# A two-stage attention and feed-forward kernel: softmax steps, the order of block sums, and the product scheme of three blocks

## The chip, the cores and the metric

One core of a Trainium2 chip runs the whole kernel. The metric is the device time of one execution in microseconds; times in the profile count from the first instruction.

## The reference

```python
def _attn_ref(q, k, v, tau):                      # q, k, v: (4, 6080, 256)
    qn = q / (np.linalg.norm(q, axis=1, keepdims=True) + 1e-06)
    kn = k / (np.linalg.norm(k, axis=1, keepdims=True) + 1e-06)
    s = kn.transpose(0, 2, 1) @ qn / tau          # 256 x 256 for each batch
    s = s - s.max(-1, keepdims=True)
    a = np.exp(s)
    a /= a.sum(-1, keepdims=True) + 1e-09
    return (v @ a).astype(np.float32)

def _moe_ref(x, w_in, w_out):                     # 256 -> 2048 -> 256
    h = np.maximum(x @ w_in, 0.0)
    return (h * h @ w_out).astype(np.float32)
```

The output is `_moe_ref` of the attention's 24320 rows.

## The kernel before

Attention here is over channels: each batch needs one 256 x 256 matrix `a` from its q and k, and `v @ a @ w_in` is computed as `v @ W` with W = `a @ w_in` made once for each batch. So a batch has an attention part (products of q and k into `gram`, sums of squares into `acc`, the softmax, W) and a feed-forward part over its tokens. The attention part of batch b + 1 is put between the steps of the feed-forward part of batch b.

**Feed-forward.** A batch's 6080 tokens are 11 blocks of 512 and one of 448. For each block, 16 steps f (128 hidden channels each) run `first_product` (line 541): six matmuls of the block's width into a PSUM tile `ps_h` (three buffers), since each float32 operand is split into a high and a low fp32r part and three of the four part products are kept, over two halves of the channels. ScalarE (ACT) applies relu into a tile `x`. Two steps make a pair r. At the odd step, `squares_and_sums` (line 565) squares the pair on ACT.

In blocks for which `by_seven` (line 534) is true, the pair is taken as a 2 x 2 arrangement of blocks, x[0] to x[3] (two hidden channel groups by two halves of the tokens), and the second product, with `w_out` arranged 2 x 2 likewise, takes seven block products in place of eight by sums of blocks: VectorE (DVE) forms x[4], x[5], x[6] and x[7] from x[0] to x[3]; ACT casts x[1] to x[3] into the first three slots of `g_hi`; DVE subtracts to get `g_lo`. The other four slots follow in `parts_of_sums` (line 582) at the next even step: a cast of x[4:8] on ACT, then `g_lo` of these on DVE. In other blocks DVE casts all of `g_hi` and subtracts once (four slots).

`second_product` (line 591) of a pair comes LAG = 2 pairs later. `seven_products` (line 612) runs three block products at an even step and four at an odd one, three matmuls each of half the block's width (256 columns for a block of 512), into two PSUM tiles `ps_o`; `eight_products` (line 668) runs six matmuls of the full width a step. At a block's last pair ACT copies `ps_o` to `o`; for seven products, `combine` (line 647) then does five additions on DVE in the odd steps 5, 7 and 9 of the next block and stores four pieces, where eight products store once.

**Attention.** `attention` (line 351) is a generator. For a chunk of q and k it casts, squares and multiplies over four calls; 25 chunks make a batch (batch 1 has 20 left). Then `softmax_and_W` (line 378) goes on: `acc` summed, `ps_n` (column sums by a product with `ones`), `nx` and a seed, three Newton rounds for the inverse square root, `nr`, then `diag` on DVE and two scalings of `gram` into `s` on ACT, `ps_b` (a product of `ones` and `diag` on TensorE), a multiplication and a maximum on DVE, two exponentials on ACT, four transposes into `ps_t`, the split of e into `eT_hi` and `eT_lo`, and W for four groups of 512 hidden channels. Each `yield` ends a call. `may_write_W` lets a group of W be written only after the last step of the batch's last block that reads the former one.

**What sets the order.** All engines keep the order of the program. The main loop (line 755) writes it by hand: from step PAIR on (the third block), the generator `beside` is called once at the start of each even step, after `first_product`, and once at the end of each odd step; steps 2 and 3 of a block have no call (line 771). So a block of 16 steps has 14 calls. Work on `v` for the next block is done at steps 6 (`split_v_hi`, ACT) and 8 (`split_v_lo`, DVE). DMAs are issued by SyncE (SP).

Of the kernel before, what the change touches and what calls it, by code (L numbers as in the profile page):

```python
# [30 lines left out]
def kernel(  # L31
# [22 lines left out]
    tensor, vector, scalar, pool_engine = (  # L54
        InProgramOrder(tc, e) for e in (nc.tensor, nc.vector, nc.scalar, nc.gpsimd)
    )
# [5 lines left out]
    T = 512  # L62
# [8 lines left out]
    blocks = []  # L71
# [141 lines left out]
    def keep_w_in(g, parts):  # L213
        for kept, part in zip(wi_kept[g], parts):
            nc.sync.dma_start(kept, part.bitcast(F32))

    def reload_w_in(b, g):
        parts = wi_tiles(b, g)
        for kept, part in zip(wi_kept[g], parts):
            nc.sync.dma_start(part.bitcast(F32), kept)  # L220
        return parts
# [129 lines left out]
    def attention(b):  # L351
# [23 lines left out]
                yield  # L375
        yield from softmax_and_W(b)

    def softmax_and_W(b):
        gram, acc = grams[b].gram, grams[b].acc
        wi = {0: reload_w_in(b, 0)} if b else {}  # L380

        vector.tensor_add(acc[:, :, 0, :], acc[:, :, 0, :], acc[:, :, 1, :])
        yield
        if b:
            yield
        ps_n = ps_h.tile([P, T], F32, tag="h", name=f"ps_n{b}")
        for m in range(2 * NC):
            tensor.matmul(
                ps_n[:, m : m + 1],
                acc[:, m // NC, 0, (m % NC) * P : (m % NC + 1) * P],  # L390
                ones[:, 0:1],
                start=m == 0,
                stop=True,
                skip_group_check=True,
            )
        yield
        yield
        small = lambda name, dt=F32: pool.tile([P, 2 * NC], dt, tag=name, name=f"{name}{b}", bufs=1)
        x = small("nx")

        vector.tensor_scalar_max(x, ps_n[:, 0 : 2 * NC], 2.0**-100)

        seed_i, y = small("nseed", I32), small("ny")
        vector.tensor_scalar(
            seed_i, x.bitcast(I32), scalar1=1, scalar2=None, op0=ALU.logical_shift_right
        )
        vector.tensor_scalar(
            y.bitcast(I32), seed_i, scalar1=-1.0, scalar2=float(0x5F3759DF), op0=ALU.mult, op1=ALU.add
        )
        s_, u_ = small("ns"), small("nu")  # L410
        yield
        for it in range(3):
            vector.tensor_mul(s_, x, y)
            vector.scalar_tensor_tensor(u_, s_, -0.5, y, op0=ALU.mult, op1=ALU.mult)
            vector.scalar_tensor_tensor(y, u_, 1.5, y, op0=ALU.add, op1=ALU.mult)
            if it == 1:
                yield
        vector.tensor_mul(s_, x, y)
        vector.tensor_scalar_add(s_, s_, 1e-6)
        vector.tensor_scalar_mul(s_[:, NC : 2 * NC], s_[:, NC : 2 * NC], tau_sb)  # L420
        r_n = small("nr")
        vector.reciprocal(r_n, s_)
        diag = pool.tile([P, NC, P], F32, tag="diag", name=f"diag{b}", bufs=1)
        for h in range(NC):
            vector.tensor_scalar_mul(diag[:, h, :], ident, r_n[:, h : h + 1])

        s = pool.tile([P, NC, C], F32, tag="s", name=f"s{b}", bufs=1)
        for h in range(NC):
            scalar.activation(s[:, h, :], gram[:, h, :], AF.Copy, scale=r_n[:, NC + h : NC + h + 1])
        yield  # L430
        yield
        ps_b = ps_h.tile([P, T], F32, tag="h", name=f"ps_b{b}")
        tensor.matmul(ps_b[:, 0:C], ones, diag.rearrange("p h c -> p (h c)"), start=True, stop=True)
        yield
        yield
        vector.tensor_mul(s, s, ps_b[:, 0:C].unsqueeze(1).broadcast_to([P, NC, C]))
        negmax = pool.tile([P, NC], F32, tag="negmax", name=f"negmax{b}", bufs=1)
        vector.tensor_reduce(negmax, s, axis=AX.X, op=ALU.max, negate=True)
        yield
        e = s  # L440
        rsum = pool.tile([P, NC], F32, tag="rsum", name=f"rsum{b}", bufs=1)
        for h in range(NC):
            scalar.activation(
                e[:, h, :], s[:, h, :], AF.Exp, bias=negmax[:, h : h + 1], accum_out=rsum[:, h : h + 1]
            )
        yield
        yield
        rinv = pool.tile([P, NC], F32, tag="rinv", name=f"rinv{b}", bufs=1)
        vector.tensor_scalar_add(rsum, rsum, 1e-9)
        vector.reciprocal(rinv, rsum)  # L450
        ps_t = ps_h.tile([P, T], F32, tag="h", name=f"ps_t{b}")
        for h in range(NC):
            for d in range(NC):
                tensor.transpose(
                    ps_t[:, d * C + h * P : d * C + (h + 1) * P], e[:, h, d * P : (d + 1) * P], ident
                )
        yield
        yield
        eT_hi = pool.tile([P, NC, C], F32R, tag="eT_hi", name=f"eT_hi{b}", bufs=1)
        eT_lo = pool.tile([P, NC, C], F32R, tag="eT_lo", name=f"eT_lo{b}", bufs=1)  # L460
        ps_tv = ps_t.rearrange("p (d c) -> p d c", d=NC)
        vector.tensor_copy(eT_hi, ps_tv)
        vector.tensor_sub(eT_lo, ps_tv, eT_hi.bitcast(F32))
        yield
        yield

        for g in range(NG):
            while (b, g) not in may_write_W:
                yield
            if b == 0:  # L470
                while g not in wi_first:
                    yield
                for _ in range(3 if g else 0):
                    yield
                hi, lo = wi_first.pop(g)
                keep_w_in(g, (hi, lo))
            else:
                hi, lo = wi.pop(g)
            w_hi = wpool.tile([P, NC, GRP], F32R, tag="w_hi", name=f"w_hi{b}_{g}")
            w_lo = wpool.tile([P, NC, GRP], F32R, tag="w_lo", name=f"w_lo{b}_{g}")  # L480
            for h in range(NC):
                ps_w = ps_h.tile([P, T], F32, tag="h", name=f"ps_w{b}_{g}_{h}")
                parts = [(d, x, y) for x, y in ((eT_hi, hi), (eT_hi, lo), (eT_lo, hi)) for d in range(NC)]
                for i, (d, et, wt) in enumerate(parts):
                    tensor.matmul(
                        ps_w[:, 0:GRP],
                        et[:, d, h * P : (h + 1) * P],
                        wt[:, d, :],
                        start=i == 0,
                        stop=i == len(parts) - 1,  # L490
                    )
                if b and h == NC - 1 and g + 1 < NG:
                    wi[g + 1] = reload_w_in(b, g + 1)
                yield
                scalar.activation(w_hi[:, h, :], ps_w[:, 0:GRP], AF.Copy, scale=rinv[:, h : h + 1])
                vector.scalar_tensor_tensor(
                    w_lo[:, h, :],
                    ps_w[:, 0:GRP],
                    rinv[:, h : h + 1],
                    w_hi[:, h, :].bitcast(F32),  # L500
                    op0=ALU.mult,
                    op1=ALU.subtract,
                )
                yield
            W[b, g] = w_hi, w_lo
            yield
# [26 lines left out]

    def by_seven(b, n):

        return blocks[n][1] == T and (b, n) > (0, 1)

    X = {}
    G = {}
# [25 lines left out]
    def squares_and_sums(b, n, r):  # L565

        x = X[b, n, r]
        G[b, n, r] = hi, lo = parts_of(b, n, r)
        seven = by_seven(b, n)
        at, src = (slice(0, 3), x[:, 1:4, :]) if seven else (slice(0, 4), x[:, 0:4, :])  # L570
        scalar.activation(x[:, 0:4, :], x[:, 0:4, :], AF.Square)
        if seven:
            vector.tensor_sub(x[:, 4:6, :], x[:, 1:3, :], x[:, 0:1, :].broadcast_to(list(x[:, 1:3, :].shape)))
            scalar.copy(hi[:, at, :], src)
            vector.tensor_add(x[:, 6, :], x[:, 2, :], x[:, 4, :])
        else:
            vector.tensor_copy(hi[:, at, :], src)
        vector.tensor_sub(lo[:, at, :], src, hi[:, at, :].bitcast(F32))
        if seven:
            vector.tensor_sub(x[:, 7, :], x[:, 3, :], x[:, 6, :])  # L580

    def parts_of_sums(b, n, r):
        x = X.pop((b, n, r))
# [126 lines left out]
    order = [(b, n) for b in range(B) for n in range(NB)]  # L710
# [3 lines left out]
    first = softmax_and_W(0)  # L714
# [40 lines left out]
    for i in range(len(steps) + 2 * LAG):  # L755
        part = now["part"] = i % 2
        if i < len(steps):
            b, n, f = steps[i]
# [19 lines left out]
        if part == 1 and i // 2 < len(pairs):  # L778
            squares_and_sums(*pairs[i // 2])
# [49 lines left out]
```

## Time and profile before

| | us |
|---|---|
| median of 3 runs | 2275.04 (2274.26 to 2276.02) |
| the profiled execution | 2274.35 |
| its span, first to last instruction | 2272.4 |
| TensorE busy in the span | 2231.8 |
| ScalarE busy | 1772.6 |
| VectorE busy | 1721.5 |

The page of the profile gives busy time by engine. The views used below it are: the windows (busy time of each engine in a stretch, with the TensorE clock granted, as a share of its full rate), the timeline (instructions in order of time, equal neighbours merged, with the idle time of the engine before one and what ended it), and the groups of instructions by shape. Matmuls overlap: what one costs in a stream is the distance between starts, not its own length. "PE" is TensorE's matmuls, "PEld" its weight loads. Every kernel instruction shows line 27, that of a helper, so rows are read by the tile's name.

### The profile page before, as it was taken

What the parts mean: (1) busy time and instruction counts of PE and PEld (TensorE: products, weight loads), DVE (VectorE), ACT (ScalarE), POOL (GpSimd) and SP (SyncE); (2) the same over time, 40 slices, a digit from 0 to 9 for tenths busy, and PEclk for the clock granted to TensorE, in tenths of its full rate; (3) what the DMA queues carried; (4) which work ended last, traced back from release to release, by engine and by line L of the source; (5) the groups of instructions that cost most, each with busy time, mean ns of one, the idle gap of its engine ahead of it and who ended that gap; (6) DMA issues with size and microseconds to landing.
All of it is one profiled execution on the core that took longest, in us unless ns stands there. A gap on an engine that the chain in (4) does not pass through costs nothing.

```text
span 2272.4 us, 33814 instructions
## 1 busy us (share of the span) xinstructions
PE 2231.8 (98%) x13524; PEld 1993.1 (88%) x13524; DVE 1721.5 (76%) x2391; ACT 1772.6 (78%) x2230; POOL 44.8 (2%) x22
## 2 busy tenths in 40 slices
PE   8899999999999999999999999999999999999999
PEld 6678999988989999998898999999889888888888
DVE  7788888877658888877766888887774677777774
ACT  5568888878668888887867888888775877877874
POOL 2130000000000000000000000000000000000000
PEclk9899999999999999999999999999999999999999
DMA  9231212100121112210021112210012010010000
GB/s 343 89 121 56 66 51 67 59 28 18 43 86 57 57 59 69 69 45 19 21 72 64 56 59 72 66 52 22 22 34 75 18 38 19 19 38 20 19 25 20
DMA packets 75581, 126.97 MB, mean 56 GB/s; under 512 B 7584, under 2 KB 33184, under 8 KB 75424
## 3 DMA queue, kind: packets, MB, share of 16 engines
q1 hardware_dynamic: 75424, 124.81, 17.0%
q8 instruction: 106, 1.74, 0.3%
q14 instruction: 51, 0.42, 0.1%
HBM read 95.68 MB, written 29.10 MB: 55 GB/s over the span
## 4 chain that ended last, share of the span: by engine, by line
PE 73%; DVE 13%; ACT 11%; issue 2%; DMA 1%; SPq 0%; DVEq 0%; ACTq 0%
PE ps_h L27 35%; PE ps_o L27 31%; DVE x L27 6%; ACT x L27 6%; PE gram L27 5%; DVE g_lo L27 4%; ACT g_hi L27 3%; PE ps_w L27 2%; DVE acc L27 1%; DVE v_lo L27 1%; ACT o L27 1%; ACT v_hi L27 1%; DMA qk<-in_k 0%; DMA w_in_raw<-in_w_in 0%; ACT s L27 0%
## 5 line engine op out<-in xcount | busy, mean ns | idle before, releaser
L27 DVE TENSOR_TENSOR g_lo<-x,g_hi 128x768 fp32r<-128x768 f32 (+2 forms) x720 | 789.2, 1096 | 172.2 <-ACT g_hi L27 166.9
L27 ACT CAST g_hi<-x 128x768 fp32r<-128x768 f32 (+1 forms) x672 | 633.4, 942 | 197.8 <-DVE x L27 182.2
L27 DVE TENSOR_TENSOR x<-x 128x256 f32<-128x256 f32 (+1 forms) x1008 | 515.7, 512 | 197.1 <-ACT x L27 185.5
L27 ACT ACTIVATE x<-ps_h 128x512 f32<-128x512 f32 (+1 forms) x768 | 453.9, 591 | 203.2 <-PE ps_h L27 200.8
L27 PE MATMUL ps_h<-v_hi,w_hi 128*128 128x512 f32 (+1 forms) x1536 | 478.7, 393 | 0.8 <-ACT w_hi L27 0.5
L27 PE MATMUL ps_h<-v_lo,w_hi 128*128 128x512 f32 (+1 forms) x1536 | 476.0, 391 | 1.7 <-DVE v_lo L27 1.7
L27 PE MATMUL ps_h<-v_hi,w_lo 128*128 128x512 f32 (+1 forms) x1536 | 476.6, 391 | 0.1
L27 ACT ACTIVATE x<-x 128x1024 f32<-128x1024 f32 (+1 forms) x384 | 404.4, 1053 | 12.2
L27 PE MATMUL ps_o<-g_lo,wS_hi 128*128 128x256 f32 x1344 | 377.6, 281 | 5.6 <-DVE g_lo L27 5.6
L27 PE MATMUL ps_o<-g_hi,wS_hi 128*128 128x256 f32 x1344 | 378.5, 282 | 1.9 <-ACT o L27 1.9
L27 PE MATMUL ps_o<-g_hi,wS_lo 128*128 128x256 f32 x1344 | 376.2, 280 | 0.0
L27 PEld LDWEIGHTS ps_h<-v_lo,w_hi 128*128 128x128 f32 x1536 | 289.0, 188 | 66.1 <-DVE v_lo L27 2.5
L27 PEld LDWEIGHTS ps_h<-v_hi,w_lo 128*128 128x128 f32 x1536 | 289.4, 188 | 62.8 <-DVE w_lo L27 0.5
L27 PE MATMUL ps_o<-g_hi,wo_hi 128*128 128x256 f32 (+2 forms) x1200 | 339.5, 296 | 0.0
L27 PE MATMUL ps_o<-g_lo,wo_hi 128*128 128x256 f32 (+2 forms) x1200 | 339.5, 296 | 0.0
L27 PE MATMUL ps_o<-g_hi,wo_lo 128*128 128x256 f32 (+2 forms) x1200 | 337.6, 294 | 0.0
L27 PEld LDWEIGHTS ps_o<-g_lo,wS_hi 128*128 128x128 f32 x1344 | 253.4, 189 | 22.5 <-DVE g_lo L27 9.2
L27 PEld LDWEIGHTS ps_o<-g_hi,wS_hi 128*128 128x128 f32 x1344 | 253.4, 189 | 20.3 <-ACT o L27 6.7
L27 PEld LDWEIGHTS ps_o<-g_hi,wS_lo 128*128 128x128 f32 x1344 | 253.9, 189 | 0.0
L27 PEld LDWEIGHTS ps_h<-v_hi,w_hi 128*128 128x128 f32 x1536 | 242.7, 189 | 9.7 <-ACT x L27 1.9
L27 PEld LDWEIGHTS ps_o<-g_lo,wo_hi 128*128 128x128 f32 x1200 | 226.0, 188 | 17.1
L27 PEld LDWEIGHTS ps_o<-g_hi,wo_hi 128*128 128x128 f32 x1200 | 225.3, 188 | 16.9
(93 smaller groups left out, 1763.9 us busy)
## 6 DMA issues: line engine op xcount, KB each, us to landing
v<-in_vT SPq DMA_DIRECT2D x44, 512.0 KB, 3.8
qk<-in_k SPq DMA_DIRECT2D x87, 256.0 KB, 2.7
qk<-in_q SPq DMA_DIRECT2D x87, 256.0 KB, 3.0
out_T<-o SPq DMA_DIRECT2D x168, 128.0 KB, 1.7
wi_lo<-wi_kept SPq DMA_DIRECT2D x12, 512.0 KB, 3.9
wi_hi<-wi_kept SPq DMA_DIRECT2D x12, 512.0 KB, 4.7
w_in_raw<-in_w_in SPq DMA_DIRECT2D x4, 1024.0 KB, 6.4
w_out_raw<-in_w_out SPq DMA_DIRECT2D x4, 1024.0 KB, 5.4
```

The lines of the kernel that those rows point to most:

```text
L27: return lambda *args, **kwargs: self.tc.keep_in_program_order(issue(*args, **kwargs))
```

## The change

Three edits. `pause` gives `softmax_and_W` a number of yields that differs for batch 0 and the others: for batch 0 all are as before; for batches 1 to 3 the calls from the sum of `acc` to the first product of W rise from 17 to 24. In `squares_and_sums` the subtraction that makes x[7] stands directly behind the addition that makes x[6], ahead of the subtraction for `g_lo`. `by_seven` becomes true for the 448-token blocks of batches 0, 1 and 2; the last block of batch 3 stays with eight products.

```diff
--- before.py
+++ after.py
@@ -375,14 +375,17 @@
                 yield
         yield from softmax_and_W(b)
 
+    def pause(b, first, other):
+
+        for _ in range(other if b else first):
+            yield
+
     def softmax_and_W(b):
         gram, acc = grams[b].gram, grams[b].acc
         wi = {0: reload_w_in(b, 0)} if b else {}
 
         vector.tensor_add(acc[:, :, 0, :], acc[:, :, 0, :], acc[:, :, 1, :])
-        yield
-        if b:
-            yield
+        yield from pause(b, 1, 2)
         ps_n = ps_h.tile([P, T], F32, tag="h", name=f"ps_n{b}")
         for m in range(2 * NC):
             tensor.matmul(
@@ -393,8 +396,7 @@
                 stop=True,
                 skip_group_check=True,
             )
-        yield
-        yield
+        yield from pause(b, 2, 2)
         small = lambda name, dt=F32: pool.tile([P, 2 * NC], dt, tag=name, name=f"{name}{b}", bufs=1)
         x = small("nx")
 
@@ -413,13 +415,13 @@
             vector.tensor_mul(s_, x, y)
             vector.scalar_tensor_tensor(u_, s_, -0.5, y, op0=ALU.mult, op1=ALU.mult)
             vector.scalar_tensor_tensor(y, u_, 1.5, y, op0=ALU.add, op1=ALU.mult)
-            if it == 1:
-                yield
+            yield from pause(b, 1 if it == 1 else 0, 1)
         vector.tensor_mul(s_, x, y)
         vector.tensor_scalar_add(s_, s_, 1e-6)
         vector.tensor_scalar_mul(s_[:, NC : 2 * NC], s_[:, NC : 2 * NC], tau_sb)
         r_n = small("nr")
         vector.reciprocal(r_n, s_)
+        yield from pause(b, 0, 1)
         diag = pool.tile([P, NC, P], F32, tag="diag", name=f"diag{b}", bufs=1)
         for h in range(NC):
             vector.tensor_scalar_mul(diag[:, h, :], ident, r_n[:, h : h + 1])
@@ -427,24 +429,22 @@
         s = pool.tile([P, NC, C], F32, tag="s", name=f"s{b}", bufs=1)
         for h in range(NC):
             scalar.activation(s[:, h, :], gram[:, h, :], AF.Copy, scale=r_n[:, NC + h : NC + h + 1])
-        yield
-        yield
+        yield from pause(b, 2, 3)
         ps_b = ps_h.tile([P, T], F32, tag="h", name=f"ps_b{b}")
         tensor.matmul(ps_b[:, 0:C], ones, diag.rearrange("p h c -> p (h c)"), start=True, stop=True)
-        yield
-        yield
+        yield from pause(b, 2, 1)
         vector.tensor_mul(s, s, ps_b[:, 0:C].unsqueeze(1).broadcast_to([P, NC, C]))
+        yield from pause(b, 0, 1)
         negmax = pool.tile([P, NC], F32, tag="negmax", name=f"negmax{b}", bufs=1)
         vector.tensor_reduce(negmax, s, axis=AX.X, op=ALU.max, negate=True)
-        yield
+        yield from pause(b, 1, 2)
         e = s
         rsum = pool.tile([P, NC], F32, tag="rsum", name=f"rsum{b}", bufs=1)
         for h in range(NC):
             scalar.activation(
                 e[:, h, :], s[:, h, :], AF.Exp, bias=negmax[:, h : h + 1], accum_out=rsum[:, h : h + 1]
             )
-        yield
-        yield
+        yield from pause(b, 2, 4)
         rinv = pool.tile([P, NC], F32, tag="rinv", name=f"rinv{b}", bufs=1)
         vector.tensor_scalar_add(rsum, rsum, 1e-9)
         vector.reciprocal(rinv, rsum)
@@ -454,15 +454,13 @@
                 tensor.transpose(
                     ps_t[:, d * C + h * P : d * C + (h + 1) * P], e[:, h, d * P : (d + 1) * P], ident
                 )
-        yield
-        yield
+        yield from pause(b, 2, 1)
         eT_hi = pool.tile([P, NC, C], F32R, tag="eT_hi", name=f"eT_hi{b}", bufs=1)
         eT_lo = pool.tile([P, NC, C], F32R, tag="eT_lo", name=f"eT_lo{b}", bufs=1)
         ps_tv = ps_t.rearrange("p (d c) -> p d c", d=NC)
         vector.tensor_copy(eT_hi, ps_tv)
         vector.tensor_sub(eT_lo, ps_tv, eT_hi.bitcast(F32))
-        yield
-        yield
+        yield from pause(b, 2, 3)
 
         for g in range(NG):
             while (b, g) not in may_write_W:
@@ -533,7 +531,7 @@
 
     def by_seven(b, n):
 
-        return blocks[n][1] == T and (b, n) > (0, 1)
+        return (0, 1) < (b, n) < order[-1]
 
     X = {}
     G = {}
@@ -573,11 +571,10 @@
             vector.tensor_sub(x[:, 4:6, :], x[:, 1:3, :], x[:, 0:1, :].broadcast_to(list(x[:, 1:3, :].shape)))
             scalar.copy(hi[:, at, :], src)
             vector.tensor_add(x[:, 6, :], x[:, 2, :], x[:, 4, :])
+            vector.tensor_sub(x[:, 7, :], x[:, 3, :], x[:, 6, :])
         else:
             vector.tensor_copy(hi[:, at, :], src)
         vector.tensor_sub(lo[:, at, :], src, hi[:, at, :].bitcast(F32))
-        if seven:
-            vector.tensor_sub(x[:, 7, :], x[:, 3, :], x[:, 6, :])
 
     def parts_of_sums(b, n, r):
         x = X.pop((b, n, r))
```

## Rows read from the trace of the kernel before

**Rows 1.** Page of the profile: busy us (share of the span) xinstructions, by engine.
```profile
PE 2231.8 (98%) x13524; PEld 1993.1 (88%) x13524; DVE 1721.5 (76%) x2391; ACT 1772.6 (78%) x2230; POOL 44.8 (2%) x22
```
**Rows 2.** Windows: stretch, us, busy PE, PEld, DVE, ACT, POOL, clock, DMA, GB/s.
```profile
480.00:506.00 26.00, 22.29 (x125) 18.66 (x125) 18.81 (x37) 16.07 (x26) 0.00 (x0) 0.93 0.13 41
1034.00:1062.00 28.00, 24.50 (x132) 20.70 (x131) 20.43 (x39) 17.55 (x27) 0.00 (x0) 0.88 0.12 38
1590.00:1616.00 26.00, 22.30 (x124) 18.60 (x123) 18.80 (x37) 16.94 (x26) 0.00 (x0) 0.93 0.14 41
...
598.00:652.00 54.00, 54.00 (x274) 48.59 (x273) 26.80 (x37) 27.77 (x42) 0.00 (x0) 1.00 0.25 78
```
**Rows 3.** Timeline, batch 3's softmax: start, us, engine, instruction, [idle before <- releaser].
```profile
1587.36 0.62 PE L27 MATMUL ps_h<-v_hi,w_hi 128*128 128x512 f32 x2
...
1608.59 0.93 PE L27 MATMUL ps_t<-ident,s 128*128 128x128 f32 x4 [1.72 <-ACT s L27]
1609.27 0.36 PE L27 MATMUL ps_o<-g_hi,wo_hi 128*128 128x256 f32 x1
...
1615.92 0.63 PE L27 MATMUL ps_h<-v_hi,w_hi 128*128 128x512 f32 x2
...
1592.59 0.84 ACT L27 ACTIVATE s<-gram,nr 128x256 f32<-128x256 f32 x2 [3.50 <-DVE nr L27]
...
1607.93 0.51 ACT L27 ACTIVATE s<-s,negmax 128x256 f32<-128x256 f32 x1 [4.13 <-DVE negmax L27]
```
**Rows 4.** Timeline of DVE, then ACT, in batch 3's feed-forward: one turn of a pair.
```profile
1878.68 1.15 DVE L27 TENSOR_TENSOR x<-x 128x512 f32<-128x512 f32 x2 [0.36 <-ACT x L27]
1879.75 0.95 DVE L27 TENSOR_TENSOR g_lo<-x,g_hi 128x768 fp32r<-128x768 f32 x1
1880.62 0.42 DVE L27 TENSOR_TENSOR x<-x 128x256 f32<-128x256 f32 x1
...
1881.07 1.05 ACT L27 CAST g_hi<-x 128x1024 fp32r<-128x1024 f32 x1 [1.06 <-DVE x L27]
...
1886.13 1.05 ACT L27 CAST g_hi<-x 128x1024 fp32r<-128x1024 f32 x1 [1.06 <-DVE x L27]
```
**Rows 5.** Timeline of PE (two pairs' starts, a wait), then ACT's copies of o.
```profile
1799.85 0.63 PE L27 MATMUL ps_h<-v_hi,w_hi 128*128 128x512 f32 x2
...
1805.08 0.63 PE L27 MATMUL ps_h<-v_hi,w_hi 128*128 128x512 f32 x2
...
1873.31 0.39 PE L27 MATMUL ps_o<-g_lo,wS_hi 128*128 128x256 f32 x1 [0.21 <-DVE g_lo L27]
...
1892.14 0.80 ACT L27 COPY o<-ps_o 128x768 f32<-128x768 f32 x1
...
2191.87 0.79 ACT L27 COPY o<-ps_o 128x768 f32<-128x768 f32 x1
```
**Rows 6.** Groups by shape, DVE: xcount | busy us, mean ns of one | idle before.
```profile
L27 DVE TENSOR_TENSOR g_lo<-x,g_hi 128x1024 fp32r<-128x1024 f32 x352 | 434.5, 1234 | 169.3 <-ACT g_hi L27 166.7
...
L27 DVE TENSOR_TENSOR g_lo<-x,g_hi 128x896 fp32r<-128x896 f32 x32 | 35.0, 1093 | 2.8
...
L27 DVE CAST g_hi<-x 128x896 fp32r<-128x896 f32 x32 | 20.1, 628 | 74.1 <-ACT x L27 74.1
```
**Rows 7.** Timeline of PE and its weight loads: distances between starts, by width.
```profile
672.20 0.28 PE L27 MATMUL ps_o<-g_hi,wo_hi 128*128 128x256 f32 x1
...
672.55 0.62 PE L27 MATMUL ps_h<-v_hi,w_hi 128*128 128x512 f32 x2
...
630.97 0.57 PE L27 MATMUL ps_h<-v_hi,w_hi 128*128 128x448 f32 x2
...
632.19 0.57 PE L27 MATMUL ps_o<-g_hi,wo_hi 128*128 128x448 f32 x2
...
1570.66 0.97 PEld L27 LDWEIGHTS ps_n<-ones,acc 128*128 128x128 f32 x8
...
39.76 2.11 PE L27 MATMUL gram<-qk 128*128 128x256 f32 x9
```

## Prediction

> **What bounds the kernel now.** I read the busy shares first. TensorE (PE) is busy for 98% of the span, VectorE (DVE) and ScalarE (ACT) for 76% and 78% [rows 1]. A share this high hides its own bubbles, since a matmul that waits for its neighbour still counts as busy; so I then read stretches. In the 448-token block of batch 0 PE is busy for all 54.00 us, and DVE and ACT for only half [rows 2]: there the number of matmuls is the time. In the three stretches where a later batch's softmax runs, PE is busy for 22.29 of 26.00, 24.50 of 28.00 and 22.30 of 26.00 us, and the granted clock falls to 0.93, 0.88 and 0.93 [rows 2]. The time goes there and, less visibly, in batch 3. These two places and the 448-token blocks are what the diff touches.
>
> The measure of "no bubble" is one pair of steps (f even, f odd) of a seven-product block: its first matmul starts at 1799.85 and that of the next pair at 1805.08, 5.23 us; a block of 8 pairs is 41.84 us [rows 5].
>
> **Part 1: x[7] before the low split (lines 571 to 580).** Nothing is added or removed, one subtraction of 128x256 moves. In batch 3 ACT and DVE form a ring: the square of a pair releases DVE's subtraction and addition (1.15 us for the two), then comes g_lo of 768 elements (0.95), then x[7] (0.42), and only then may ACT cast the 1024 elements of the second g_hi; it sat idle 1.06 us for that [rows 4]. ACT is in order, so the next relu and the next square queue behind that cast. The ring turns in 1886.13 - 1881.07 = 5.06 us [rows 4]. That is less than PE's 5.23, but a block also puts two copies of o, the split of v and four additions of `combine` on it. The copy of o comes every (2191.87 - 1892.14)/7 = 42.82 us in batch 3, against PE's 41.84 [rows 5]. So the ring bounds batch 3, by 0.98 us a block. PE first waits at 1873.31 us, for a g_lo [rows 5]; from there to the last 512-token block are 8 blocks: 7.8 us. With x[7] first, the 0.95 leaves the ring: some 4.1 us a pair, 34 a block and a few us for the extras, well below 41.84. Late next is PE itself. The price: g_lo of 768 ends about 0.35 us later; it is read two pairs (10 us) later, so nothing waits. I take 7.8; the ends are 0 (rival 4) and 7.8.
>
> **Part 2: softmax of batches 1 to 3 over 24 calls in place of 17.** In batch 3, PE's step 6 of the block starts at 1587.36 and step 14 at 1615.92 [rows 3]: 28.56 us for four pairs, 7.64 over 4 x 5.23. Of this PE needs some itself: the four transposes take 1609.27 - 1608.59 = 0.68 [rows 3], the product with `ones` about 0.46 (two instructions at the rate of f32 products, 2.11/9 = 0.23 each [rows 7]). About 6.5 us are lost. The rows show how: ACT reaches the two scalings of `s` and sits idle 3.50 us for `nr`, the last of a train of tiny DVE instructions; later it sits idle 4.13 us for `negmax`, with the relu of the next step queued behind the exponentials; PE, two steps ahead, meets the transposes and waits 1.72 us [rows 3], then again for a g_lo that is late for the same reason. After that PE runs at the lower of its two levels (1.2 of 2.4 GHz): a mean of 0.93 over 26 us is 3.6 us at half speed, some 1.8 us lost, which is inside the 6.5 [rows 2].
>
> Batch 1 has the same busy time and clock, so the same 6.5. Batch 2 has 0.88 of 28 us: 6.7 us at the lower level, 3.1 more, hence 1.5 us more, less 0.2 of shorter idle: 7.8 [rows 2]. Sum 20.8 us.
>
> What the new steps do, by position in the block (calls fall on the start of an even step and on the end of an odd one; steps 2 and 3 have none). The first Newton round falls on step 4, the second on 5, the third on 6, the four closing instructions on 7, `diag` and `s` on 8, `ps_b` at the end of 11, the multiplication on 12, the maximum on 13, the exponentials on 15, the transposes on 5 of the next block, the eT split on 6. So ps_b comes three calls after diag (now two), the exponentials two after the maximum (now one, after both DVE instructions), the transposes four calls and one call-free pair after the exponentials (now two). The 4.13 us wait and the transposes' 1.72 should be gone, and with them the fall of the clock. What stays: `s` still follows `nr` by one call, and on DVE the second piece of `combine`, the four closing instructions and, just behind, v_lo crowd steps 7 to 9. ACT will still wait there, 2.5 to 3.5 us; the hi cast, lo split and relus behind it then come close to PE's need for them. The same 3.50 us wait now ends in stalls of PE of about 0.6 us each, which left the clock alone. I leave two such stalls in each batch, 1.2 us, so 3.6 of 20.8 stays: gain 17.2. The ends: 0.3 stays in each batch (19.9), or half of all stays (10.4). The seven extra calls cost nothing at the end of the softmax: W may be written only in the batch's last block; a batch of 12 blocks has 14 calls in each, and 25 chunks of 4 calls and 24 more are 124 of the 154 before its last block (batch 1, which starts two blocks late with 20 chunks: 104 of 126). The queues that the moved steps pass: the reload of w_in is issued ahead of the first of them and does not move; SP and POOL see no change of order. Batch 0 keeps its pauses.
>
> **Part 3: seven products in three of the 448-token blocks.** Second product before: 16 x 3 x 2 = 96 matmuls of 448 columns, six of which start within 632.19 - 630.97 = 1.22 us, 0.2033 each: 19.5 us a block [rows 7]. After: 8 x 7 x 3 = 168 matmuls of 224 columns. No row has that width for fp32r operands. By columns alone it is half of 0.2033: 17.1 us, gain 2.4 a block. But each matmul needs a weight load of its own, and where matmuls are as short as one column, eight loads take 0.97 us, (0.97 - 0.19)/7 = 0.111 apart [rows 7]: 168 x 0.111 = 18.7, gain 0.8. At 256 columns starts lie (672.55 - 672.20)/3 = 0.117 apart [rows 7]; if 224 columns do no better, 19.7, loss 0.1. I take 0.111, because it is the only row in which a weight load and not a stream of columns sets the pace, and it lies above the 0.102 of the columns: 2.4 us for three blocks, ends -0.4 and 7.3.
>
> The Trainium skill ("TensorE: Matmul & The Clock Gate", LDWEIGHTS (loading the stationary operand)) gives a load as its columns divided by 1.2, 107 ns for 128, whatever the matmul behind it, a rule that speaks against narrow matmuls; by it the three blocks would gain 4.6 us, where the row's 0.111 gives 2.4; the trace has no such load behind a matmul of 224 columns, and its nearest case is 4% slower than the rule.
>
> Added beside PE, per pair: DVE trades 0.63 + 1.09 [rows 6] for 1.15 + 0.42 + 0.95 + 1.23 at most (durations of the wider block [rows 4, 6]), so +2.0, 16.3 a block and 2.6 for `combine`: 26.80 + 19 = 46 of 54 us. ACT gains two casts, at most 1.05 each [rows 4], 16.8, and a wider copy of o: 27.77 + 18 = 46 of 54 [rows 2]. Both stay under PE, so this hides; without the cover it would be 1 us per pair. Four output DMAs of half the width replace one of both; PE does not wait for them.
>
> **Sum.** 7.8 + 17.2 + 2.4 = 27.4. The profiled execution took 2274.35 us (its span is 2272.4): 2246.95. The median of the runs is 2275.04, 0.69 above: forecast 2247.6.
>
> **The rivals.**
> 1. Slower: a matmul of 224 fp32r columns runs at the rate of plain f32. For it speaks only that no row shows this width; against it that 512, 448 and 256 columns all run at about 2.2 columns per ns. Price: an f32 product of 256 columns is two instructions 0.23 apart [rows 7], 0.46; for 224 columns 0.40; 168 x 0.40 = 67 against 19.5, +48 a block, +144 in all. With the 25.0 of parts 1 and 2: 2275.0 + 119 = 2394. It decides from an interval of (25.0 + 3 x 19.5)/504 = 0.166 us on.
> 2. Columns alone set the pace of the 224-column matmuls (0.102): gain 7.8 + 17.2 + 7.3 = 32.3, 2242.7. For it: from 448 to 256 columns the interval shrinks in proportion. The skill's same page (Back-to-back issue gap) has columns over 2.4 plus 2.5 ns, 96 ns; by that, 2239.8; the 448-column row is 0.203 against its 0.189, so the trace does not bear it out.
> 3. The waits only move: the crowd on DVE at steps 7 to 9 keeps ACT late, half of the softmax's loss stays, and 224 columns gain nothing: 7.8 + 10.4 - 0.4 = 17.8, 2257.2. For it: the wait for `nr` is still one call long.
> 4. The reorder does nothing, because ACT would then wait for the PE's relu input or for the pair's own 768 cast: 19.6, 2255.4. Against it: the 1.06 us wait is for x[7] and nothing else.
> 5. The spread does not do what it says: PE stalls and the clock falls as before, because it is the order on ACT and not the distance in calls that binds: 10.2, 2264.8.
>
> **How the numbers follow.** Forecast 0.44, rival 1 0.09, rival 2 0.20, rival 3 0.12, rival 4 0.06, rival 5 0.06, no change at all 0.03. Range 2239 to 2262: it holds the forecast and rivals 2, 3 and 4, 0.82, and reaches the largest sum (7.8 + 19.9 + 7.3 = 35.0, 2240.0). A measurement of this kernel tells 0.2% (4.6 us) from no change. Faster by more: all but rival 1 and no change, 0.88; within 0.2%: 0.03; slower: 0.09.
>
> **What the profile after would show.** Part 1: in batch 3 ACT no longer idles for x before its cast of 1024, its copies of o come every 41.8 us, and PE has no wait for o or g_lo. Part 2: clock 1.00 in the three stretches, no wait of PE for `s` at the transposes; a wait of ACT for `nr` left. Part 3: ps_o of 128x224, 504 of them, starting 0.10 to 0.12 apart; their interval is the number that would prove me most wrong. If the clock still falls, part 2 is wrong; if the copies of o stay at 42.8, part 1.

## The result

| | before | after |
|---|---|---|
| median of the runs, us | 2274.65 (4 runs, 2274.11 to 2276.02) | 2241.64 (4 runs, 2241.43 to 2242.01) |
| span of the profiled execution, us | 2272.4 | 2239.7 |
| TensorE busy, us | 2231.8 | 2211.0 |

The ratio is 0.9854, 95% interval 0.9837 to 0.9871: 33.0 us less. The forecast was 2247.6 (range 2239 to 2262).

The traces say where they went, block by block: a block's time is the distance between the first matmuls (`ps_h`) of two neighbouring blocks on PE.

| part | forecast, us | measured in the traces, us |
|---|---|---|
| batch 3's ring (blocks 2 to 10) | 7.8 | 8.4 |
| three softmax stretches (blocks 8 to 10 of batches 0 to 2) | 17.2 | 6.6 + 7.7 + 6.7 = 21.0 |
| three 448-token blocks, with the block behind each | 2.4 | 0.99 + 0.99 + 0.97 = 2.95 |
| the first 180 us and the last block | 0 | 0.5 |

All other blocks agree within 0.03 us. The last line is no effect of the change: the part ahead of the third block, with the same code there, came out between 1.3 us shorter and 0.7 us longer than before in the kernels of this study.

### The profile page after: what moved, and what is told of

It reads as the page before. It is cut to its first block, busy times and chain, and to the rows that moved or that the text cites. A ratio compares the mean times of both kernels' runs of the same rounds, so it can differ in the third digit from the quotient of the medians.

```text
span 2239.7 us, 34384 instructions
## 1 busy us (share of the span) xinstructions
PE 2211.0 (99%) x13740; PEld 1989.4 (89%) x13740; DVE 1784.1 (80%) x2478; ACT 1833.7 (82%) x2278; POOL 44.8 (2%) x22
## 3 DMA queue, kind: packets, MB, share of 16 engines
q1 hardware_dynamic: 76336, 124.81, 17.2%
## 4 chain that ended last, share of the span: by engine, by line
PE 93%; DVE 4%; ACT 1%; DMA 1%; issue 1%; SPq 0%; DVEq 0%
PE ps_h L27 45%; PE ps_o L27 41%; PE gram L27 5%; PE ps_w L27 2%; DVE acc L27 1%; DVE g_lo L27 1%; DMA qk<-in_k 0%; ACT x L27 0%; DVE x L27 0%; DMA w_in_raw<-in_w_in 0%; DVE dec_e L27 0%; DMA w_out_raw<-in_w_out 0%; DVE o L27 0%; PE ps_n L27 0%; DVE g_hi L27 0%
## 5 line engine op out<-in xcount | busy, mean ns | idle before, releaser
L27 DVE TENSOR_TENSOR g_lo<-x,g_hi 128x768 fp32r<-128x768 f32 (+2 forms) x744 | 808.9, 1087 | 60.4 <-ACT g_hi L27 57.9
L27 DVE TENSOR_TENSOR x<-x 128x256 f32<-128x256 f32 (+3 forms) x1080 | 551.6, 511 | 279.8 <-ACT x L27 254.7
L27 ACT CAST g_hi<-x 128x768 fp32r<-128x768 f32 (+1 forms) x720 | 674.1, 936 | 23.2 <-DVE x L27 10.3
L27 PE MATMUL ps_o<-g_hi,wS_hi 128*128 128x256 f32 (+1 forms) x1440 | 402.9, 280 | 0.0
L27 PE MATMUL ps_o<-g_lo,wS_hi 128*128 128x256 f32 (+1 forms) x1440 | 401.7, 279 | 0.3
L27 PE MATMUL ps_o<-g_hi,wS_lo 128*128 128x256 f32 (+1 forms) x1440 | 401.9, 279 | 0.0
L27 PE MATMUL ps_o<-g_lo,wo_hi 128*128 128x256 f32 (+3 forms) x1176 | 331.7, 289 | 0.0
L27 PE MATMUL ps_o<-g_hi,wo_hi 128*128 128x256 f32 (+3 forms) x1176 | 331.3, 288 | 0.0
L27 PE MATMUL ps_o<-g_hi,wo_lo 128*128 128x256 f32 (+3 forms) x1176 | 329.9, 287 | 0.0
L27 PEld LDWEIGHTS ps_o<-g_lo,wS_hi 128*128 128x128 f32 x1440 | 271.2, 188 | 15.2 <-DVE g_lo L27 0.9
L27 PEld LDWEIGHTS ps_o<-g_hi,wS_lo 128*128 128x128 f32 x1440 | 271.8, 189 | 0.0
L27 PEld LDWEIGHTS ps_o<-g_hi,wo_hi 128*128 128x128 f32 x1176 | 221.1, 188 | 15.3
```

What stands on the lines that cost most here:

```text
L27: return lambda *args, **kwargs: self.tc.keep_in_program_order(issue(*args, **kwargs))
```

## The profile after

Page, busy us by engine [rows 1]:

```profile
PE 2211.0 (99%) x13740; PEld 1989.4 (89%) x13740; DVE 1784.1 (80%) x2478; ACT 1833.7 (82%) x2278; POOL 44.8 (2%) x22
```

Windows over the three softmax stretches (the later two shifted with the work) and over batch 0's 448-token block [rows 2]; columns as there:

```profile
480.00:506.00 26.00, 25.89 (x162) 23.10 (x161) 23.43 (x43) 20.88 (x27) 0.00 (x0) 1.00 0.13 41
1026.00:1054.00 28.00, 27.88 (x177) 25.00 (x176) 25.35 (x47) 22.88 (x34) 0.00 (x0) 1.00 0.12 39
1573.00:1599.00 26.00, 25.89 (x161) 23.09 (x160) 23.38 (x44) 20.88 (x28) 0.00 (x0) 1.00 0.14 41
590.00:644.00 54.00, 54.00 (x348) 50.16 (x347) 38.21 (x61) 40.31 (x57) 0.00 (x0) 1.00 0.24 78
```

PE now idles 0.11 us where it idled 3.7, and the clock stays at its upper level. In the 448-token block DVE and ACT rise from 27 and 28 to 38 and 40 us and stay under PE.

Timeline of the softmax of batch 3 [rows 3]: ACT's scalings and exponentials, then PE's transposes.

```profile
1580.48 0.84 ACT L27 ACTIVATE s<-gram,nr 128x256 f32<-128x256 f32 x2 [2.44 <-DVE nr L27]
...
1598.91 0.51 ACT L27 ACTIVATE s<-s,negmax 128x256 f32<-128x256 f32 x1
...
1613.34 0.60 PE L27 MATMUL ps_t<-ident,s 128*128 128x128 f32 x4
1613.69 0.48 PE L27 MATMUL ps_h<-v_hi,w_hi 128*128 128x512 f32 x1
```

The exponentials and the transposes no longer wait (4.13 and 1.72 us before). The wait for `nr` is left, 2.44 us. The four transposes now pass in 0.35 us, half of what they took behind the stall.

Timeline of one pair in batch 3, DVE and then ACT, and ACT's copies of o six blocks apart [rows 4, 5]:

```profile
1904.19 1.61 DVE L27 TENSOR_TENSOR x<-x 128x512 f32<-128x512 f32 x3 [1.27 <-ACT x L27]
1905.72 0.95 DVE L27 TENSOR_TENSOR g_lo<-x,g_hi 128x768 fp32r<-128x768 f32 x1
...
1905.25 0.60 ACT L27 ACTIVATE x<-ps_h 128x512 f32<-128x512 f32 x1 [0.22 <-PE ps_h L27]
1905.83 1.05 ACT L27 CAST g_hi<-x 128x1024 fp32r<-128x1024 f32 x1
1906.79 0.79 ACT L27 COPY o<-ps_o 128x768 f32<-128x768 f32 x1
...
2157.67 0.79 ACT L27 COPY o<-ps_o 128x768 f32<-128x768 f32 x1
```

All three instructions that form the sums of blocks come before g_lo, ACT's cast does not wait, and it is ACT that waits for PE. The copies come every (2157.67 - 1906.79)/6 = 41.81 us: the 41.84 of eight pairs at 5.23 us, to a rounding.

Timeline of PE in a 448-token block: one odd step's end and the start of its twelve 224-column matmuls [rows 7]:

```profile
620.64 0.27 PE L27 MATMUL ps_o<-g_hi,wS_hi 128*128 128x224 f32 x1
620.75 0.28 PE L27 MATMUL ps_o<-g_lo,wS_hi 128*128 128x224 f32 x1
...
621.97 0.63 PE L27 MATMUL ps_w<-wi_hi,eT_hi 128*128 128x512 f32 x2
```

Twelve take 1.33 us, 0.111 each.

Two rows serve for the experiments: PE at the first matmul of block 8 and of block 11 (the 448-token block) of batch 2, of the kernel before and then of the changed one. Between them lies the softmax for batch 3.

```profile
1571.58 0.48 PE L27 MATMUL ps_h<-v_hi,w_hi 128*128 128x512 f32 x1
1705.19 0.36 PE L27 MATMUL ps_h<-v_hi,w_hi 128*128 128x448 f32 x1
```

```profile
1554.86 0.48 PE L27 MATMUL ps_h<-v_hi,w_hi 128*128 128x512 f32 x1
1681.75 0.36 PE L27 MATMUL ps_h<-v_hi,w_hi 128*128 128x448 f32 x1
```

133.61 us before, 126.89 after. In the other kernels this distance is called the softmax blocks' time.

## The experiments

Theory: three independent parts, a ring in batch 3, a softmax whose steps follow each other in too few calls, and a weight load that sets the pace of 224 columns. The main rival on the softmax: it is not the distance in calls. The runs were made in three groups, each with runs of the kernel before beside it (medians 2274.45 to 2275.01); differences to the changed kernel are to its 2241.64.

**1. The order alone.**

```diff
+            vector.tensor_sub(x[:, 7, :], x[:, 3, :], x[:, 6, :])
         else:
             vector.tensor_copy(hi[:, at, :], src)
         vector.tensor_sub(lo[:, at, :], src, hi[:, at, :].bitcast(F32))
-        if seven:
-            vector.tensor_sub(x[:, 7, :], x[:, 3, :], x[:, 6, :])
```

> The kernel before with x[7] moved ahead of the low split, nothing else. Theory (ring): the copies of o in batch 3 come every 41.8 us instead of 42.82, 8.4 us off the whole, about 2266; the three softmax stretches keep their stalls and the clock still falls there. Rival (the ring also keeps ScalarE late ahead of the softmax, so that the order and not the distance in calls decides there too): much of the softmax's 21 us goes as well, 2255 or less, and the clock stays at 1.00 in those stretches.

Measured: 2262.52 us, ratio 0.9948 (0.9933 to 0.9963), 11.9 us less. Blocks 3 to 9 of batch 3 take 41.81 us, 8.4 us off in all: the ring is confirmed. The softmax stretch stays (timeline of PE):

```profile
1568.81 0.48 PE L27 MATMUL ps_h<-v_hi,w_hi 128*128 128x512 f32 x1
...
1605.40 0.44 PE L27 MATMUL ps_t<-ident,s 128*128 128x128 f32 x2 [1.87 <-ACT s L27]
...
1608.09 0.58 PE L27 MATMUL ps_o<-g_lo,wS_hi 128*128 128x256 f32 x1 [0.87 <-DVE g_lo L27]
...
1701.36 0.36 PE L27 MATMUL ps_h<-v_hi,w_hi 128*128 128x448 f32 x1
```

132.55 us against 133.61: the wait at the transposes is still there (1.87 us), the clock of that stretch is still 0.93, and only 1.1 us went (0.6 and 1.9 in the other two batches). The rival, that the order frees the softmax too, falls for the order alone.

**2. The longer pauses alone.** The diff's `pause` lines on the kernel before, nothing else.

> The kernel before with the longer pauses alone. Theory (distance in calls): the three softmax stretches lose nearly all of their 6.6, 7.7 and 6.7 us, 2254; batch 3's blocks stay at 42.8 us. Rival (order): with the ring still in place ScalarE and VectorE stay late, TensorE still waits for s at the transposes or for g_lo, half or less is gained, 2264 or more.

Measured: 2259.27 us, ratio 0.9933 (0.9920 to 0.9947), 15.2 us less.

```profile
1561.12 0.48 PE L27 MATMUL ps_h<-v_hi,w_hi 128*128 128x512 f32 x1
...
1590.81 0.39 PE L27 MATMUL ps_o<-g_lo,wS_hi 128*128 128x256 f32 x1 [0.88 <-DVE g_lo L27]
...
1619.61 0.39 PE L27 MATMUL ps_o<-g_hi,wS_hi 128*128 128x256 f32 x1 [0.25 <-ACT o L27]
...
1690.28 0.36 PE L27 MATMUL ps_h<-v_hi,w_hi 128*128 128x448 f32 x1
```

129.16 us: two thirds of the 6.7 go, and the clock stays at 1.00. Neither expectation holds. What is left, 2.3 us, is a late g_lo and, from block 9 on, waits for ACT's copy of o: the sign of the ring, which now bounds the two blocks behind the softmax as it bounds batch 3 (whose blocks stay at 42.80).

**3. Seven products alone.** Only the line of `by_seven`.

> The kernel before with seven products in the 448-token blocks of batches 0 to 2 alone. Theory (a weight load of 0.111 us sets the pace of the 224-column matmuls): 168 x (0.111) against 96 x 0.2038 gives 0.9 to 1.0 us a block, 3 us off, 2272. Rival (columns alone, 0.102): 2.4 us a block, 2267.5. Rival (the ring, with w_hi and w_lo on it, bounds these blocks): no gain or a loss.

Measured: 2269.95 us (11 runs, 2268.43 to 2270.96), ratio 0.9981 (0.9972 to 0.9989), 4.5 us less. The three 448-token blocks with the block behind each give 3 x 0.98 us as in the changed kernel; 1.0 us lies ahead of the third block, where the code is the same; the last 0.5 us lies between the medians and the two profiled executions, in no block of the traces. The softmax blocks' times add up to what they were (0.1 us more), but not batch by batch: 1.4 us more, 1.1 less and 0.2 less. How long the clock stays down after a stall is not tied to the batch (windows of the first two stretches, clock the third number from the end):

```profile
480.00:506.00 26.00, 22.29 (x119) 18.63 (x118) 18.79 (x37) 17.02 (x26) 0.00 (x0) 0.90 0.13 41
1034.00:1062.00 28.00, 25.06 (x142) 21.22 (x141) 20.39 (x39) 18.59 (x28) 0.00 (x0) 0.94 0.12 38
```

Here batch 1's softmax has the longer fall, in the kernel before it was batch 2's (0.88) [rows 2].

**4. Changed kernel, old order.** The two pieces of the first diff reversed.

> The changed kernel with x[7] behind the low split again (pauses and sevens kept). Theory (parts add): 8.4 us slower than the changed kernel, all of it in batch 3, 2250. Rival (the spread softmax needs the shorter ring): stalls come back in the softmax stretches too, 2255 or more, with a lower clock there.

Measured: 2257.15 us, 15.5 more than the changed kernel; ratio to before 0.9924 (0.9911 to 0.9938).

```profile
1560.79 0.48 PE L27 MATMUL ps_h<-v_hi,w_hi 128*128 128x512 f32 x1
...
1689.98 0.36 PE L27 MATMUL ps_h<-v_hi,w_hi 128*128 128x448 f32 x1
```

129.19 us. So the pauses win 2.3 us in each of three batches, 6.9, only together with the order, which alone won 0.6 to 1.9 there (run 1); with batch 3's 8.4 that is 15.3 of the 15.5. The parts do not simply add, though the clock stays up, where the rival had it fall.

**5. Changed kernel, late half close again.** ps_b two calls after diag, then two calls to multiplication and maximum in one call, the exponentials one call later, the transposes two calls after these.

```diff
-        yield from pause(b, 0, 1)
         negmax = pool.tile([P, NC], F32, tag="negmax", name=f"negmax{b}", bufs=1)
         vector.tensor_reduce(negmax, s, axis=AX.X, op=ALU.max, negate=True)
-        yield from pause(b, 1, 2)
+        yield from pause(b, 1, 1)
...
-        yield from pause(b, 2, 4)
+        yield from pause(b, 2, 2)
```

> The changed kernel with the late half of the softmax close again: ps_b two calls after diag, multiplication and maximum in one call, the exponentials one call later, the transposes two calls after these; the early half keeps its spread. Theory (distance): TensorE waits 1.5 to 2 us at the transposes and runs at the lower clock level behind it, 4 to 5 us a batch, 12 to 15 us slower than the changed kernel, about 2255. Rival (order): with x[7] early ScalarE has the slack, 1 us slower or less, 2242.

Measured: 2241.30 us, ratio to before 0.9851 (0.9836 to 0.9866): the time of the changed kernel.

```profile
1554.06 0.48 PE L27 MATMUL ps_h<-v_hi,w_hi 128*128 128x512 f32 x1
...
1596.85 0.60 PE L27 MATMUL ps_t<-ident,s 128*128 128x128 f32 x4
...
1680.94 0.36 PE L27 MATMUL ps_h<-v_hi,w_hi 128*128 128x448 f32 x1
...
1593.40 0.50 ACT L27 ACTIVATE s<-s,negmax 128x256 f32<-128x256 f32 x1
```

126.88 us, no wait at the transposes. My theory, distance counted in calls, falls here: with the calls that the kernel before had, the stall is gone. Two things differ. One is the place: multiplication and maximum stand on step 12; in the kernel before they stood on step 9, where DVE also has the third piece of `combine` and, just ahead, v_lo. The other I overlooked: one call is not always the same distance. From the end of step 9 to the start of step 10 ACT has a single relu between maximum and exponentials, and it waits 4.13 us [rows 3]; from the start of step 12 to the end of step 13 a pair's work stands between them, and ACT does not wait. So distance counted in work is not refuted by this run.

**6. Changed kernel, early half close again.** Newton rounds as before, `diag` and `s` behind the closing instructions in the same call (on step 5), so that all that follows, though spread, falls on steps 8 to 12.

```diff
-            yield from pause(b, 1 if it == 1 else 0, 1)
+            yield from pause(b, 1 if it == 1 else 0, 1 if it == 1 else 0)
...
-        yield from pause(b, 0, 1)
         diag = pool.tile([P, NC, P], F32, tag="diag", name=f"diag{b}", bufs=1)
```

> The changed kernel with the early half close again: two Newton rounds in one call, the third with the four closing instructions, diag and s in the next; the late half keeps its spread. Theory (distance): ScalarE waits about 3.5 us for nr as in the kernel before, but ps_b is three calls away; TensorE loses 0.5 to 1.5 us a batch to a late g_lo, 2243 to 2246, no fall of the clock. Rival: the early spread carries half of the gain, 2250 or more.

Measured: 2250.05 us, ratio to before 0.9889 (0.9873 to 0.9906), 8.4 more than the changed kernel.

```profile
1560.65 0.48 PE L27 MATMUL ps_h<-v_hi,w_hi 128*128 128x512 f32 x1
...
1584.99 0.38 PE L27 MATMUL ps_o<-g_lo,wS_hi 128*128 128x256 f32 x1 [0.55 <-DVE g_lo L27]
...
1597.75 0.39 PE L27 MATMUL ps_o<-g_lo,wS_hi 128*128 128x256 f32 x1 [1.53 <-DVE g_lo L27]
...
1690.17 0.36 PE L27 MATMUL ps_h<-v_hi,w_hi 128*128 128x448 f32 x1
```

129.52 us, 2.6 a batch. PE waits for a late g_lo, not at the transposes, and the clock stays at 1.00. The rival's number came true, not the theory's. ACT waits 3.63 us for `nr` as in run 1 (3.62), 2.44 in the changed kernel: the spread of the early half is worth 2.6 us a batch by itself. So three theories were left: the place (steps 5 to 10 are crowded), the distance in the early half, or both.

**7. Old distances, later place.** The 17-call pauses, with six more calls ahead of the Newton rounds.

```diff
-        yield
+        yield from pause(b, 1, 7)
         for it in range(3):
```

> The changed kernel with the 17-call distances of the kernel before in batches 1 to 3, but six more calls ahead of the Newton rounds: the closing instructions, diag and s fall on the end of step 11, ps_b on 13, multiplication and maximum on 15, the exponentials on step 0 of the next block, the transposes on 4. Theory (place: what hurts is that these stand on steps 5 to 10, where VectorE also has combine and the split of v): no wait of TensorE above 0.5 us, the clock stays at 1.00, 2241 to 2243. Theory (distance in calls): the waits for nr, at the transposes and the lower clock come back, 4 to 6 us a batch, 2254 to 2260.

Measured: 2246.98 us, ratio 0.9876 (0.9861 to 0.9891), 5.3 more than the changed kernel.

```profile
1558.03 0.48 PE L27 MATMUL ps_h<-v_hi,w_hi 128*128 128x512 f32 x1
...
1609.94 0.39 PE L27 MATMUL ps_o<-g_lo,wS_hi 128*128 128x256 f32 x1 [0.88 <-DVE g_lo L27]
...
1686.69 0.36 PE L27 MATMUL ps_h<-v_hi,w_hi 128*128 128x448 f32 x1
...
1594.56 0.84 ACT L27 ACTIVATE s<-gram,nr 128x256 f32<-128x256 f32 x2 [3.71 <-DVE nr L27]
...
1606.60 0.51 ACT L27 ACTIVATE s<-s,negmax 128x256 f32<-128x256 f32 x1 [2.50 <-DVE negmax L27]
```

128.66 us, between the two theories. From run 1 (order, old distances, old place) to here 3.9 us of 5.7 went with the place; 1.8 stayed with the closeness. ACT's wait for `nr` is 3.71 us, and here, where the maximum again ends a step and the exponentials begin the next, it waits 2.50 us for the maximum (4.70 in run 1, none in run 5); PE's wait for g_lo comes 3 us later.

**8. New distances, crowded place.** The changed kernel with ten more calls at the same spot.

```diff
-        yield
+        yield from pause(b, 1, 11)
         for it in range(3):
```

> The changed kernel with ten more calls ahead of the Newton rounds, all its other distances kept: diag and s fall on step 4 of the next block, ps_b on 7, the multiplication on 8, the maximum on 9, the exponentials on 11. Theory (place): VectorE is crowded there, g_lo comes late, TensorE loses 1 to 3 us a batch, 2245 to 2251. Theory (distance): nothing changes, 2241 to 2242.

Measured: 2240.87 us (2239.30 to 2241.48), ratio 0.9847 (0.9831 to 0.9864).

```profile
1555.12 0.48 PE L27 MATMUL ps_h<-v_hi,w_hi 128*128 128x512 f32 x1
...
1681.57 0.36 PE L27 MATMUL ps_h<-v_hi,w_hi 128*128 128x448 f32 x1
...
1610.14 0.84 ACT L27 ACTIVATE s<-gram,nr 128x256 f32<-128x256 f32 x2
```

126.45 us, 0.4 less than the changed kernel, no wait of PE, as the distance theory had it. The place alone does no harm: the same crowded steps take the late half one instruction at a time. And ACT does not wait for `nr`: the call-free steps 2 and 3 now stand between `nr` and `s`.

**9. Order, and the split of v moved.** Run 1 with `split_v_hi` and `split_v_lo` at steps 10 and 12; the softmax has its old pauses and place.

```diff
-            at_hi, at_lo = (None, None) if at == 0 else (13, 14) if at == 1 else (6, 8)
+            at_hi, at_lo = (None, None) if at == 0 else (13, 14) if at == 1 else (10, 12)
```

> The kernel before with x[7] early (as the first run of this study, 2262.5) and, beside it, the split of v for the next block at steps 10 and 12 in place of 6 and 8; the softmax keeps its 17 calls and its place. Theory (place): the cast and the subtraction of v (1.05 us on ScalarE, 1.22 us on VectorE) no longer stand ahead of the maximum, which comes over 1 us sooner; 1.5 to 4 us a batch are won, 2250 to 2258. Theory (distance): the wait at the transposes stays, 2262.

Measured: 2255.16 us, ratio 0.9912 (0.9897 to 0.9927), 7.4 less than run 1.

```profile
1564.15 0.48 PE L27 MATMUL ps_h<-v_hi,w_hi 128*128 128x512 f32 x1
...
1598.68 0.33 PE L27 MATMUL ps_t<-ident,s 128*128 128x128 f32 x1 [0.28 <-ACT s L27]
...
1601.37 0.39 PE L27 MATMUL ps_o<-g_lo,wS_hi 128*128 128x256 f32 x1 [0.88 <-DVE g_lo L27]
...
1694.15 0.36 PE L27 MATMUL ps_h<-v_hi,w_hi 128*128 128x448 f32 x1
```

130.00 us against 132.55: no softmax line was touched, the wait at the transposes falls from 1.87 to 0.28 us, and the clock stays at 1.00. But 3.1 of run 1's 5.7 us stay, and ACT still waits 3.57 us for the maximum (4.70 in run 1). Runs 5 to 9 agree on one reading: with little work between a step and the one that needs it, ACT waits, and the crowd of `combine` and the split of v makes that wait longer. Only where both meet does PE wait over 1 us at the transposes and the clock fall. Spreading the steps takes away the whole loss, in the crowd (run 8) and outside it (run 5); moving the two apart takes away 3.9 of 5.7 us (run 7) or 2.6 (run 9).

**10. Other widths.** The second and third matmul of each product narrowed, which leaves part of the products out.

```diff
+                rows, cols = P, half
+                if i:
+                    if tn < T:
+                        rows, cols = ((64, half), (P, 160), (P, 192))[b]
+                    elif b == 3 and 4 <= n <= 6:
+                        rows = 64
                 tensor.matmul(
-                    ps[:, at, :half],
-                    wt,
-                    gt[:, slot, :],
+                    ps[:rows, at, :cols],
+                    wt[:, :rows],
+                    gt[:, slot, :cols],
```

> The changed kernel with, in seven_products, the second and third matmul of each product narrowed in four places: 448-token block of batch 0: weights of 64 columns in place of 128, still 224 columns streamed; batch 1: 160 columns streamed; batch 2: 192 streamed (both with 128 weight columns); 512-token blocks 4 to 6 of batch 3: weights of 64 columns, 256 streamed. That part of the products is left out. Theory (the load of 128 weight columns sets 0.111 us): batch 1 and 2 stay at 0.111 to 0.112 between the second and third start, batch 0 falls to 0.100 to 0.103. At 256 columns 0.117 should stay, if there columns set the pace, or fall toward 0.110 if loads do. Rival (columns with a fixed cost each): batch 1 falls to about 0.083, batch 2 to 0.097, batch 0 stays at 0.111.

Measured (one execution; timeline of PE, batch 1: two products of three matmuls, then the next step; then the first matmuls of batch 1's 448-token block and of the block behind it):

```profile
1155.67 0.31 PE L27 MATMUL ps_o<-g_hi,wS_hi 128*128 128x224 f32 x1
1155.82 0.25 PE L27 MATMUL ps_o<-g_lo,wS_hi 128*128 128x160 f32 x1
1155.90 0.27 PE L27 MATMUL ps_o<-g_hi,wS_lo 128*128 128x160 f32 x1
1156.01 0.31 PE L27 MATMUL ps_o<-g_hi,wo_hi 128*128 128x224 f32 x1
...
1134.27 0.36 PE L27 MATMUL ps_h<-v_hi,w_hi 128*128 128x448 f32 x1
1179.68 0.43 PE L27 MATMUL ps_h<-v_hi,w_hi 128*128 128x512 f32 x1
```

The starts bunch: 0.15, 0.08 and 0.11 us. The second-to-third distance is 0.083 on average, the number that I had put down for the rival: by that sign alone the theory would be out. But the sign was badly chosen, since the distance ahead of it grows to 0.131 on average: three starts take 0.34 us here and 0.32 on average, where columns alone would need 3 x 0.111 x (224 + 160 + 160)/(3 x 224) = 0.27 if they had set the pace before. And the block takes 45.41 us with 160 columns, 45.38 with 192, against 45.40 with 224: fewer columns buy nothing. Half as many weight columns do: batch 0's block takes 44.71, 0.69 less, and the block behind it 0.23 less; its starts lie 0.105 apart on average. So the pace is that of one weight load of 128 columns per matmul, 0.111 us, and single starts move about it. In batch 3 the narrower weights bought nothing at 256 columns (blocks of 41.91 to 41.95 against 41.81; why they are 0.1 longer is not shown): there columns set the pace.

## Why the prediction was right, and where it was not

**The ring (part 1).** Right, and by its own step: the cast no longer waits, ACT waits for PE, 41.81 us a block. It was mis-sized at 7.8 for 8.4: I counted eight blocks at 0.98. Seven gave 1.00 each, the last 0.77, and the block in which PE first waits, not counted, 0.65. Rival 4 is out (run 1). The step that failed is that the order has no say elsewhere: "Late next is PE itself" was argued for batch 3 alone, and runs 2 and 4 show 2.3 us a batch behind the softmax that the pauses win only with the order.

**The softmax (part 2).** The sum of what could be won, 20.8, was about right (21.0 went, and run 8 wins 0.4 more a batch); the 3.6 us that I kept back for two stalls of 0.6 a batch were too much. The wait for `nr` stayed, 2.44 us and so just under the 2.5 to 3.5 of the forecast, and costs PE one short stall: two starts 0.39 us apart, where 0.12 is the rule. The reason was right in kind, since spreading removes the waits, but I counted the distance in calls, and that step failed. I wrote that the 4.13 us wait and the transposes' 1.72 should be gone because the exponentials come two calls after the maximum and the transposes four after them. Run 5 takes all of these calls back and loses nothing; what it keeps is a pair's work between maximum and exponentials. I had named the crowd of steps 7 to 9, and put it only on the side of what would remain: runs 7 and 9 show that it made up 2.6 to 3.9 of the 5.7 us, and run 8 that it costs nothing once the steps are spread. And the early half, of which I expected a wait of about the old length to remain, is worth 2.6 us a batch (run 6, where that wait is 3.63 us). Batch 2 was given 1.3 us more than the others, as the trace had it; run 3 shows that this is how long the clock happened to stay down, not a trait of the batch.

**The 448-token blocks (part 3).** Right in its choice among three rows: 0.111 us, taken from the loads behind one-column matmuls, is what 224 columns show, and run 10 shows why. The gain is 0.98 a block for 0.8, and the term that was mis-sized is the 448 columns: the 0.2033 of [rows 7] is the distance of the first product's matmuls (`ps_h`), while the 96 of the second product (`ps_o`) lie 0.206 apart on average in the same trace, 19.7 us, which makes the sum 1.1 against 168 x 0.111 = 18.6. The work on DVE and ACT hides, as costed (38 and 40 of 54 us, under the bound of 46). Rival 2 forecast 2242.7, nearest to the measured time, and is wrong all the same: its 4.9 us are not in these blocks, and 3.8 us of the miss lie in the softmax. Run 10 has starts 0.108 to 0.111 us apart on average with one load of 128 columns each, for 160 to 224 columns of the matmul. The Trainium skill ("TensorE: Matmul & The Clock Gate", LDWEIGHTS (loading the stationary operand)) gives a load as its columns over 1.2, 107 ns for 128; the trace's 0.111 agrees to 4%.

**The rest.** Rival 1 is out: 224 fp32r columns run at no special rate. Rival 3 is out: PE idles 0.11 us in the stretch. Rival 5 is out, since the stalls and the fall of the clock are gone; its ground, that the distance in calls does not bind, holds for the late half (run 5). The forecast lay 6.0 us above the time: 3.8 from the softmax, 0.6 each from the ring and the 448-token blocks, the rest from the first 180 us and the difference of the medians. Two readings were off without weight in the sum: `combine` has five additions, not four, and the f32 instructions of [rows 7] start 0.215 us apart, where 2.11/9 counts the last one's own length too.

Still open: whether `combine` alone, without the split of v, makes a crowd; its three steps were not moved. Nor was a kernel run with the early half spread and the exponentials directly behind the maximum, so how the loss of run 1 divides between the two halves is argued from the waits and not shown.

## What to carry to other kernels

Where engines keep program order, measure how far a step stands from its producer by the work that the engines have in between, not by the calls of a generator: here one call was a pair's work or a single relu. Then ask what else the engines have to do in that stretch: moving other work away cured a part of the stall of PE, spreading the steps cured it. A ring between two engines that is a little faster than the bound engine still costs something as soon as other work sits on it: look for it in the time of a block, not in busy shares. And halving a matmul's columns to save products paid here only down to the time of its weight load.

## What the runs showed of the hardware that I had not expected

The stream of matmuls that is bound by its weight loads did not start evenly in run 10: with 160 columns between 224-column ones, starts lay 0.08 to 0.15 us apart about a mean of 0.108, against 0.111 with 224 columns alone. The granted clock fell in part of each softmax stretch of the kernel before, where PE idled 3.7 of 26 us (mean 0.93 of 2.4 GHz [rows 2]), and of runs 1 and 3; in run 2, where PE waited only for g_lo and for o, it stayed at 1.00, as it did in run 6 with a single wait of 1.53 us. How long it stayed at the lower level differed between batches of the same code (0.90 and 0.94 in run 3, 0.93 and 0.88 before), so a difference between such stretches is no trait of the batch.
